# The first key tile loaded ahead of the MLP and query weights in a gated decode step

## The chip, the cores and the metric

One NeuronCore of a Trainium2 chip runs the whole program. The metric is the device time of one execution in microseconds (us). A core has five engines with their own instruction streams: PE (TensorE, matrix products into PSUM; its weight loads are listed as PEld), DVE (VectorE), ACT (ScalarE), POOL (GpSimd) and SP (SyncE), which here only issues loads. Sixteen DMA engines move data between the chip's memory (HBM) and the on-chip memory (SBUF). In this text a row of the page or of a timeline reads: line of the kernel, engine, operation, output <- inputs, shapes, count.

## The reference

One token goes through two branches, which a gate mixes. Branch A is attention over the last 4096 positions of a key and value cache with 16 key heads and 32 query heads of 128; branch B is a dense layer of 4608 with GELU.

```python
x = A_x                                           # [1, 1, 576]
g = sigmoid((x * gate_w).sum(-1, keepdims=True))
# A: W = 4096, rep = 2
q = (x @ wq).reshape(B, Sq, 32, 128).transpose(0, 2, 1, 3)
k = repeat(k_cache[:, :, Sk - W:, :], 2, axis=1)  # cache [1, 16, 32768, 128]
v = repeat(v_cache[:, :, Sk - W:, :], 2, axis=1)
p = softmax(einsum("bhqd,bhkd->bhqk", q, k) * 128 ** -0.5)
o = einsum("bhqk,bhkd->bhqd", p, v)
a = o.transpose(0, 2, 1, 3).reshape(1, 1, 4096) @ wo       # wo [4096, 576]
# B: w1 [576, 4608], w2 [4608, 576]
b = gelu(x @ w1 + b1) @ w2 + b2
return g * a + (1 - g) * b
```

All inputs and the output are bf16. Some 53.6 MB of weights and cache are read once; the output is one row of 576.

## The kernel before, in words

**Tiles and buffers.** The large loads share four SBUF buffers, named by a tag: A, B, C and D. A later tile with the same tag takes the place of the earlier one and can be loaded only when the earlier one has been read for the last time.

- A: the query weights wq (L234), then key tile 3, then value tile 2.
- B: w1 (L230), then key tile 2, then both halves of w2.
- C: key tile 0, then value tile 0, then value tile 3.
- D: key tile 1, then value tile 1, then wo.

A key or value tile holds four of the sixteen heads (`HB = 4`, so there are `NG = 4` tiles of each): 128 partitions with 128 positions of 128 numbers, 4096 KB. It is loaded by one DMA from SP in `load` (L533 to L539); each partition is one contiguous row of the cache, and the source's pattern walks 32 position blocks and 4 heads.

**The order of the loads.** SP issues in program order: w1 in two parts (L233), wq (L237), key tiles 0 to 3 (`load` called from `transpose`, L545), value tiles 0 and 1, the first half of w2 (L646), value tile 2, the small rest of wo (L651), value tile 3, wo (L752), and the second half of w2 in four parts (L757). An issue that has to wait for its buffer holds up all issues behind it. `first_load_ahead` (L48 to L59) takes the first DMA that SP has in the body of the program and puts it ahead of the barrier at the program's start, so that one load is issued at once. ACT issues four small loads of x, gate_w, b2 and b1 (L224 to L227).

**Stages.** (1) x is spread over partitions (L336 to L352) and the gate computed (L356 to L378). `y_add` (L386) starts the output sum in PSUM with the bias b2. (2) The w1 products (`moved`, L407, called at L426 and L427) and the turn of their result (`turned`, L432) give GELU and the vector `gt`. (3) The wq products (L407, called at L484), the turn `q_turned` on DVE (L487), one product (L492) and four copies on ACT (L505) put the queries into `qz_flat`. (4) For each key tile and each half f of it, DVE transposes the half in 32 by 32 blocks (`transpose`, L550) into a buffer `kt`, and PE makes 16 score products from it (`score_products`, L572). `row_max`, `exps` and `probs` (L588 to L621) make the softmax of a tile while the next one is worked on. (5) `value_products` (L662) for each value tile, with sums and the per-head output (L676 to L697). (6) The products of `gt` with w2 and of the attention output with wo (L386), two narrow casts (L828, L829), and the store (L830).

**Small buffers.** `kt_pool` has two buffers, used in turn by `rows`, `turned`, `q_turned` and then the `kt` halves. So the first `kt` half takes the buffer of `turned`, the second that of `q_turned`, and the third waits until the score products of the first are done.

**Order on the engines.** The helper `queue` (L526) ties each PE and DVE instruction from stage 4 on to the one before it, so the order on those engines is the order in which the code is written:

```python
transpose(0, 0)
scores(0, 0)
transpose(0, 1)
scores(0, 1)
for g in range(1, NG):
    transpose(g, 0)
    scores(g, 0)
    ...
```

Of the kernel before, what the change touches and what calls it, by code (L numbers as in the profile page):

```python
# [10 lines left out]
BF16 = mybir.dt.bfloat16  # L11
# [7 lines left out]
def kernel(  # L19
# [15 lines left out]
    nc = tc.nc  # L35

    P = 128
    D = 576
    Hq, Hkv, Dh = 32, 16, 128
    Sk, W = 32768, 4096  # L40
    HB = 4
    NG = Hkv // HB
    NKP = P // HB
    NCK = W // NKP
# [165 lines left out]
    big = ctx.enter_context(tc.tile_pool(name="big", bufs=1, side="right"))  # L210
# [16 lines left out]
    nc.scalar.dma_start(out=b1_t, in_=B_b1.rearrange("(h n) -> h n", h=2))  # L227


    w1_t = big.tile([P, NI, FH], BF16, name="w1_t", tag="B")  # L230
    w1_src = B_w1.rearrange("d (h n) -> (d h) n", h=2).rearrange("(p i) n -> p i n", i=NI)
    for i0, i1 in ((0, 4), (4, NI)):
# [11 lines left out]
    for base, pattern, keep in (  # L244
# [15 lines left out]
        out=is0[:], in0=low[:], scalar1=0.0, scalar2=None, op0=ALU.is_equal  # L260
# [15 lines left out]
        out=at31,  # L276
        in_=at31,
# [8 lines left out]
        out=hi5[:],  # L286
        in_=ones[:, 0:5],
# [7 lines left out]
        out=hi5[:],  # L295
        in_=hi5[:],
# [9 lines left out]
        out=hi16[:], in0=is0[:, c0 : c0 + 16], scalar1=-SCALE, scalar2=None, op0=ALU.mult  # L306
# [6 lines left out]
        out=row_of,  # L313
        in_=row_of,
# [9 lines left out]
        out=foreign[:],  # L324
        in_=foreign[:],
# [11 lines left out]
        out=xdup.rearrange("p (d t) -> p d t", t=2),  # L337
        in_=x_row.rearrange("p (d o) -> p d o", o=1).to_broadcast([1, D, 2]),
    )
    xs_ps = ps_m.tile([P, NI, 1], FP32, name="xs_ps", tag="m")  # L340
    for i in range(NI):
# [9 lines left out]
        out=x2[:, :, 0:2], in0=xs_ps[:].to_broadcast([P, NI, 2]), in1=alt, op=ALU.mult  # L351
# [5 lines left out]
        out=junk_row,  # L357
# [72 lines left out]
    for c0, src, q in ((0, h_s[0], 2), (1024, h_s[1], 2), (2048, h_m, 4)):  # L430
        n = 1024 if q == 2 else 256
        nc.vector.transpose(  # L432
            out=turned[:, c0 : c0 + n],
            in_=src[:].rearrange("p (q l j) -> p q j l", q=q, l=32),
# [13 lines left out]
    for q in range(4):  # L448
        quad = slice(32 * q, 32 * q + 32)
        nc.scalar.copy(  # L450
            out=hacc[quad], in_=hp_ps[quad, q, :, :].rearrange("p t j -> p (t j)")
# [6 lines left out]
        out=poly[:],  # L458
# [15 lines left out]
        out=gt[:], in0=hacc[:], scalar=omg[:, 0:1], in1=r_t[:], op0=ALU.mult, op1=ALU.mult  # L474
# [11 lines left out]
    for c in range(2):  # L486
        nc.vector.transpose(  # L487
            out=q_turned[:, 1024 * c : 1024 * c + 1024],
            in_=q_s[c][:].rearrange("p (h l b) -> p h b l", l=32, b=2),
# [9 lines left out]
    for b in range(4):  # L499
# [6 lines left out]
            out=diag[:, :, :, 0:8],  # L506
            in_=qj_ps[quad].rearrange("p j g q -> p g j q"),
# [18 lines left out]
    def queue(engine, emit):  # L526
        if engine in issued:
            with tc.issue_after(issued[engine].ins):
                issued[engine] = emit()
        else:  # L530
            issued[engine] = emit()

    def load(name, tag, cache, g):  # L533
        tile_ = big.tile([P, NCK, Dh], BF16, name=name, tag=tag)
        src = cache[0, HB * g : HB * g + HB, Sk - W : Sk, :].rearrange(
            "b (k c) d -> k b (c d)", k=NKP
        )
        nc.sync.dma_start(out=tile_[:].rearrange("p c d -> p (c d)"), in_=src)
        return tile_  # L539

    k_t, s_ps, kt = [None] * NG, [None] * NG, {}

    def transpose(g, f):
        if f == 0:
            k_t[g] = load("k_t", "CDBA"[g], A_k_cache, g)  # L545
        kt[g, f] = kt_pool.tile([P, SL * Dh], BF16, name="kt", tag="kt")
        keys = k_t[g][:, f * SL : (f + 1) * SL, :]
        queue(
            "dve",
            lambda: nc.vector.transpose(  # L550
                out=kt[g, f][:].bitcast(FP32),
                in_=keys.rearrange("p c d -> p (c d)").bitcast(FP32),
            ),
        )
# [63 lines left out]
    def probs(g):  # L618
# [6 lines left out]
# [9 lines that stand above are left out]
        if g > 1:  # L634
            probs(g - 2)
        row_max(g - 1)
        transpose(g, 1)
        scores(g, 1)
        exps(g - 1)
# [3 lines left out]
    w2_t = big.tile([P, NF, D], BF16, name="w2_t", tag="B")  # L643
    w2_src = B_w2.rearrange("(b p j) n -> p b j n", b=2, j=NJ)
    v_t = [load("v_t", "CD"[g], A_v_cache, g) for g in range(2)]
    nc.sync.dma_start(out=w2_t[:, 0:NJ, :], in_=w2_src[:, 0])  # L646
    v_t.append(load("v_t", "A", A_v_cache, 2))
    wo_src = A_wo.rearrange("(h d) n -> h d n", d=P)
    tail = wo_src[:, 4 * RW : P, :]
    for h0, h1, at, k in ((0, 16, 0, 4), (16, Hq, 32, 4)):  # L650
        load_tail = nc.sync.dma_start(  # L651
            out=wo_tail[at : at + h1 - h0].rearrange("h j n -> h (j n)"),
            in_=tail[h0:h1].rearrange("h j n -> h (j n)"),
# [40 lines left out]
    def outputs(g):  # L694
# [19 lines left out]
        out=ls[:],  # L714
# [22 lines left out]
        out=rgh[:],  # L737
# [15 lines left out]
        out=wo_t[:].rearrange("p r n -> p (r n)"),  # L753
        in_=wo_src[:, 0 : 4 * RW, :].rearrange("h (a r) n -> h a (r n)", a=4),
# [4 lines left out]
    def w2_rows(f0, f1):  # L759
        for f in range(f0, f1):  # L760
# [9 lines left out]
            out=om_t.rearrange("p (u h) -> p u h", u=2)[:, :, 0:16],  # L770
# [8 lines left out]
            out=om[:], in0=o_all.to_broadcast([P, Hq, 4]), in1=rgh[:, :, 0:4], op=ALU.mult  # L779
# [81 lines left out]
```

## Time and profile before

Three runs took 131.43, 131.53 and 131.67 us, median 131.53. The profiled execution took 131.67 us; the profile's span, from the first to the last recorded instruction, is 130.3 us.

| | busy us | share of the span |
|---|---|---|
| PE (matmul) | 79.3 | 61% |
| DVE | 61.0 | 47% |
| PEld (weight load) | 26.2 | 20% |
| ACT | 11.5 | 9% |
| POOL | 10.0 | 8% |
| DMA queue of SP's loads, of 16 engines | | 96.3% |

HBM was read at 412 GB/s over the span. The TensorE clock that the throttle granted was 0.82 of full speed on average. The busy shares are means over stages that have different limits; in a slice row each digit is the busy share of one fortieth of the span, in tenths. PE waited 15.1 us in all before score products, and 12.0 us before value products for their tiles to land. DVE waited 4.8 us in two pieces for key tiles.

### The profile page before, as it was taken

How to read it: one execution, taken by the hardware profiler on the slowest of the kernel's cores; microseconds unless marked ns; L12 is line 12 of the kernel's file. 1: busy time of each engine (PE TensorE's matmuls, PEld its weight loads, DVE VectorE, ACT ScalarE, POOL GpSimd, SP SyncE). 2: the span in 40 equal slices, each digit the busy share in tenths (PEclk: the TensorE clock that was granted, in tenths of full speed). 3: DMA queues.
4: the chain of work that ended last, by engine and by line, in shares of the span. 5: the costliest groups of instructions: out<-in, count | busy, mean ns of one | idle time of the engine just before them, and what ended most of it. 6: DMA issues, size and time to landing. Idle time of an engine off the chain costs nothing.

```text
span 130.3 us, 1142 instructions
## 1 busy us (share of the span) xinstructions
PE 79.3 (61%) x538; PEld 26.2 (20%) x412; DVE 61.0 (47%) x50; ACT 11.5 (9%) x27; POOL 10.0 (8%) x32
## 2 busy tenths in 40 slices
PE   0003899297106996859949946995300840789794
PEld 0003012110100221211211210132200320245572
DVE  0030006215199769999999995145900050051001
ACT  3032100300300000030003003003000000000001
POOL 7009800100000000000000000000010000000000
PEclk9999999658755799985999995599655577579999
DMA  7999999899899999989989989999989999898970
GB/s 249 404 437 432 475 419 475 364 473 473 362 453 473 408 402 473 433 382 473 443 372 473 453 362 473 391 458 443 443 372 477 444 392 475 384 493 356 407 294 15
DMA packets 2503, 53.67 MB, mean 412 GB/s; under 512 B 286, under 2 KB 418, under 8 KB 708
## 3 DMA queue, kind: packets, MB, share of 16 engines
q1 hardware_dynamic: 2490, 53.61, 96.3%
q8 instruction: 3, 0.05, 0.2%
q10 hardware_dynamic: 10, 0.01, 0.0%
HBM read 53.62 MB, written 0.00 MB: 412 GB/s over the span
## 4 chain that ended last, share of the span: by engine, by line
DMA 60%; DVE 21%; PE 13%; issue 5%; ACT 0%; DVEq 0%
DMA k_t<-in_A_k_cache_dram 31%; DMA wo_t<-in_A_wo_dram 25%; DVE kt L550 15%; PE y_ps L386 5%; PE s_ps L572 5%; DMA rows<-in_A_x_dram 5%; DVE m L588 3%; DVE pt L621 2%; PE s_ps L662 1%; PE acc L662 1%; DVE mr L591 1%; ACT out_row L828 0%; PE mt_ps L597 0%; DVE negm L605 0%; DVEq L550 0%
## 5 line engine op out<-in xcount | busy, mean ns | idle before, releaser
L572 PE MATMUL s_ps<-kt,qz_flat 128*128 128x512 bf16 x128 | 35.3, 436 | 15.1 <-DVE kt L550 8.3
L550 DVE STREAM_TRANSPOSE kt<-k_t 128x4096 f32<-128x4096 f32 x8 | 35.3, 4432 | 4.8 <-DMA k_t<-in_A_k_cache_dram 4.8
L662 PE MATMUL s_ps<-v_t,pt 128*32 128x512 bf16 x96 | 9.1, 547 | 12.0 <-DMA v_t<-in_A_v_cache_dram 12.0
L572 PEld LDWEIGHTS <-qz_flat 128*128 128x128 bf16 x64 | 7.2, 112 | 40.6 <-issue 40.4
L676 DVE TENSOR_TENSOR own<-s_ps,is 128x512 f32<-128x512 f32 x3 | 2.1, 688 | 18.9 <-PE s_ps L662 18.9
L609 ACT ACTIVATE p_t<-s_ps,negm 128x1024 bf16<-128x1024 f32 x4 | 4.5, 1114 | 50.0 <-DVE negm L605 50.0
L662 PEld LDWEIGHTS <-pt 128*32 128x32 bf16 x128 | 3.7, 117 | 17.5 <-DMA v_t<-in_A_v_cache_dram 12.2
L342 PE MATMUL xs_ps<-ident,rows 1*128 1x1 bf16 x9 | 0.6, 189 | 10.8 <-POOL ident masks.py:199 10.8
L407 PE MATMUL s_ps<-w_t,x 128*32 128x512 bf16 x36 | 6.0, 611 | 1.6 <-DVE x L350 1.6
L588 DVE TENSOR_REDUCE m<-s_ps 128x1 f32<-128x1024 f32 x4 | 4.8, 1195 | 3.9 <-PE s_ps L572 3.9
L386 PE MATMUL y_ps<-w_t,gt 128*1 128x272 bf16 (+1 forms) x72 | 6.3, 304 | 0.0
L407 PE MATMUL s_ps<-wq_t,x 128*32 128x512 bf16 x36 | 4.9, 619 | 2.2 <-DMA wq_t<-in_A_wq_dram 2.2
L621 DVE STREAM_TRANSPOSE pt<-p_t 128x1024 bf16<-128x1024 bf16 x4 | 4.9, 1224 | 2.7 <-ACT p_t L609 2.7
L432 DVE STREAM_TRANSPOSE turned<-s_ps 128x1024 f32<-128x1024 f32 x2 | 2.5, 1249 | 7.3 <-PE s_ps L407 7.2
L829 DVE CAST out_row<-y_ps 1x272 bf16<-1x272 f32 x1 | 0.4, 429 | 10.2 <-PE y_ps L386 10.2
L713 POOL TENSOR_TENSOR ls<-is,sums 128x32 f32<-128x32 f32 x1 | 0.2, 240 | 63.9 <-ACT p_t L609 63.9
L697 PE MATMUL mt_ps<-is,summed 128*128 128x8 f32 x8 | 2.0, 319 | 4.6 <-DVE summed L686 4.6
L386 PE MATMUL y_ps<-wo_t,ov 128*1 128x272 bf16 (+1 forms) x62 | 4.2, 286 | 0.8 <-DMA wo_t<-in_A_wo_dram 0.8
L356 DVE CUSTOM_DVE_ANT_0 rows<-rows 1x576 bf16<-1x576 bf16 x1 | 0.7, 746 | 8.3 <-DMA rows<-in_gate_w_dram 8.3
L386 PEld LDWEIGHTS <-gt 128*1 128x1 bf16 x72 | 4.0, 89 | 1.9 <-issue 0.7
L686 DVE TENSOR_REDUCE summed<-own 128x128 f32<-128x512 f32 x4 | 4.2, 1044 | 0.1
L487 DVE STREAM_TRANSPOSE q_turned<-s_ps 128x1024 f32<-128x1024 f32 x2 | 2.4, 1228 | 3.8 <-PE s_ps L407 3.8
(83 smaller groups left out, 51.9 us busy)
## 6 DMA issues: line engine op xcount, KB each, us to landing
k_t<-in_A_k_cache_dram SPq DMA_DIRECT2D x4, 4096.0 KB, 33.9
v_t<-in_A_v_cache_dram SPq DMA_DIRECT2D x4, 4096.0 KB, 22.8
wq_t<-in_A_wq_dram SPq DMA_DIRECT2D x1, 4608.0 KB, 25.0
wo_t<-in_A_wo_dram SPq DMA_DIRECT2D x1, 4464.0 KB
w_t<-in_B_w_dram SPq DMA_DIRECT2D x1, 2880.0 KB, 14.4
w_t<-in_B_w_dram SPq DMA_DIRECT2D x1, 2592.0 KB, 23.6
w_t<-in_B_w_dram SPq DMA_DIRECT2D x1, 2304.0 KB, 8.3
w_t<-in_B_w_dram SPq DMA_DIRECT2D x1, 1440.0 KB
```

Of the source, the lines that this page charges most:

```text
L386: last = nc.tensor.matmul(y_out[s], lhsT=vec, rhs=row[:, DH:D] if s else row[:, 0:DH], start=start, stop=stop, skip_group_check=True,)
L407: nc.tensor.matmul(last[n][32 * g : 32 * g + 32], lhsT=vec, rhs=part(n), start=start and g0 == 0, stop=g0 + 4 + g >= len(pieces), skip_gro ...
L432: nc.vector.transpose(out=turned[:, c0 : c0 + n], in_=src[:].rearrange("p (q l j) -> p q j l", q=q, l=32),)
L487: nc.vector.transpose(out=q_turned[:, 1024 * c : 1024 * c + 1024], in_=q_s[c][:].rearrange("p (h l b) -> p h b l", l=32, b=2),)
L550: lambda: nc.vector.transpose(out=kt[g, f][:].bitcast(FP32), in_=keys.rearrange("p c d -> p (c d)").bitcast(FP32),),
L572: last = nc.tensor.matmul(s_ps[g][:, u * 512 : (u + 1) * 512].rearrange("p (c k) -> p c k", k=32), lhsT=qz(g, j, 2 * f + half), rhs=kv[:, ...
L588: queue("dve", lambda: nc.vector.reduce_max(out=m1[:], in_=s_ps[g][:], axis=AX.X))
L609: nc.scalar.activation(out=p_t[:].rearrange("p c k -> p (c k)"), in_=s_ps[g][:], func=ACT.Exp, bias=negm[:, 0:1], scale=SCALE, accum_out=s ...
L621: lambda: nc.vector.transpose(out=pt[:, g, :, :].rearrange("p c q -> p (c q)"), in_=p_t[:].rearrange("p c k -> p (c k)"),),
L662: last = nc.tensor.matmul(acc[g][32 * (c % 4) : 32 * (c % 4) + 32, :], lhsT=pt[:, g, c, :], rhs=v_t[g][:, c:NCK:32, :], start=(c < 4), sto ...
L676: lambda: nc.vector.tensor_tensor(out=own[:], in0=acc[g].rearrange("p (c d) -> p c d", c=4), in1=same_c.rearrange("p (c o) -> p c o", o=1) ...
L686: lambda: nc.vector.tensor_reduce(out=summed[g][:], in_=own[:].rearrange("p c d -> p d c"), axis=AX.X, op=ALU.add,),
```

## The change

`load` is defined earlier, and key tile 0 is loaded with it ahead of w1 and wq. `transpose` loads the other three as before. Nothing else in the program's text differs.

```diff
     nc.scalar.dma_start(out=b1_t, in_=B_b1.rearrange("(h n) -> h n", h=2))
 
 
+    def load(name, tag, cache, g):
+        tile_ = big.tile([P, NCK, Dh], BF16, name=name, tag=tag)
+        src = cache[0, HB * g : HB * g + HB, Sk - W : Sk, :].rearrange(
+            "b (k c) d -> k b (c d)", k=NKP
+        )
+        nc.sync.dma_start(out=tile_[:].rearrange("p c d -> p (c d)"), in_=src)
+        return tile_
+
+    k_t = [None] * NG
+    k_t[0] = load("k_t", "C", A_k_cache, 0)
     w1_t = big.tile([P, NI, FH], BF16, name="w1_t", tag="B")
...
-    def load(name, tag, cache, g):
...
-    k_t, s_ps, kt = [None] * NG, [None] * NG, {}
+    s_ps, kt = [None] * NG, {}
 
     def transpose(g, f):
-        if f == 0:
+        if f == 0 and g > 0:
             k_t[g] = load("k_t", "CDBA"[g], A_k_cache, g)
```

SP's order becomes key tile 0, w1, w1, wq, key tiles 1 to 3, and then as before. The load that `first_load_ahead` puts ahead of the barrier is now key tile 0, and both parts of w1 are issued behind the barrier. In the program that comes out, DVE, ACT and POOL have the same instructions in the same order. On PE the products that start the output sum with b2 (L386) stand ahead of all w1 products, where before five w1 products with four weight loads stood ahead of them; there are four weight loads fewer, since weights that are still loaded are not loaded again (`keep_weights`).

More of the change, by code (lines that the diff above doesn't have):

```diff
@@ L531, in queue @@
             issued[engine] = emit()
-    def load(name, tag, cache, g):
[L534 to L539, printed above, removed]
-    k_t, s_ps, kt = [None] * NG, [None] * NG, {}
+    s_ps, kt = [None] * NG, {}
     def transpose(g, f):
-        if f == 0:
+        if f == 0 and g > 0:
             k_t[g] = load("k_t", "CDBA"[g], A_k_cache, g)
```

## The prediction

> **What bounds the kernel now.** I read the busy rows first, then the windows, then the chain of waits, then the rows of the stage that the change touches. The page's second part:
>
> ```profile
> DVE  0030006215199769999999995145900050051001
> PEclk9999999658755799985999995599655577579999
> DMA  7999999899899999989989989999989999898970
> ```
>
> The DMA row stands at 8 or 9 from the second slice to the last but two; DVE is full only in the middle. Windows give it sharply (columns: stretch, its length, busy time of PE, PEld, DVE, ACT, POOL, then clock, DMA share, GB/s):
>
> ```profile
> 0.00:0.90 0.90, 0.00 (x0) 0.00 (x0) 0.00 (x0) 0.00 (x0) 0.21 (x5) 1.00 0.00 0
> 0.90:1.10 0.20, 0.00 (x0) 0.00 (x0) 0.00 (x0) 0.00 (x0) 0.20 (x3) 1.00 2.75 553
> ...
> 4.00:124.00 120.00, 74.73 (x474) 23.08 (x350) 60.61 (x49) 9.83 (x25) 7.21 (x15) 0.80 1.00 430
> 124.00:126.00 2.00, 2.00 (x37) 1.62 (x33) 0.00 (x0) 0.00 (x0) 0.00 (x0) 1.00 0.88 353
> 126.00:128.00 2.00, 2.00 (x32) 1.30 (x29) 0.00 (x0) 0.00 (x0) 0.00 (x0) 1.00 0.29 108
> ```
>
> The transfer engines start about 1.0 us after the first issue and are then busy without a hole, at 430 GB/s, for 120 us. The chain of waits (start, length, what) tells another story until its last lines:
>
> ```profile
> 46.65 4.45 DVE kt L550
> ...
> 79.34 0.07 DVE negm L605
> 79.41 6.44 PE s_ps L572 x16
> ...
> 89.91 32.07 DMA wo_t<-in_A_wo_dram
> 121.97 0.04 issue
> 122.01 6.60 PE y_ps L386 x90
> ```
>
> wo_t is 4464 KB (KB here are 1024 bytes), which at 430 GB/s is 10.6 us of data, yet it lands 32.07 us after its issue: for 21 us it only stood behind earlier transfers. So the chain's DVE links, which release that issue, have slack, and what sets the end is the byte count: start of the stream, bytes, then the 6.6 us of y_ps products.
>
> The stage that is touched, in the timeline:
>
> ```profile
> 26.18 4.91 PE L407 MATMUL s_ps<-wq_t,x 128*32 128x512 bf16 x36 [2.22 <-DMA wq_t<-in_A_wq_dram]
> ...
> 30.67 2.38 DVE L487 STREAM_TRANSPOSE q_turned<-s_ps 128x1024 f32<-128x1024 f32 x2 [3.76 <-PE s_ps L407]
> ...
> 35.88 8.77 DVE L550 STREAM_TRANSPOSE kt<-k_t 128x4096 f32<-128x4096 f32 x2 [2.83 <-DMA k_t<-in_A_k_cache_dram]
> ...
> 40.38 8.97 PE L572 MATMUL s_ps<-kt,qz_flat 128*128 128x512 bf16 x32 [6.78 <-DVE kt L550]
> ...
> 46.65 4.45 DVE L550 STREAM_TRANSPOSE kt<-k_t 128x4096 f32<-128x4096 f32 x1 [2.00 <-DMA k_t<-in_A_k_cache_dram]
> ```
>
> DVE waits 2.83 us for key tile 0 and 2.00 us for key tile 1; between them it runs.
>
> **The change, part by part.**
>
> *Bytes.* Nothing is added or dropped. w1 (2304 + 2880 KB), wq (4608 KB) and key tile 0 (4096 KB) come in the order key, w1, w1, wq. What follows them has the same bytes ahead of it as before, so key tile 1 and every later load keep their place in the stream. One 4096 KB tile is 9.75 us at 430 GB/s; the two landings in the timeline, wq at 26.18 and key tile 0 at 35.88, are 9.70 us apart.
>
> *Landings.* The first half of w1, 8.3 us from its issue to landing before, moves to about 18.0; the second, landed at 0.80 + 14.4 = 15.2, to 24.9; wq takes key tile 0's old landing, 35.88. Key tile 0 is there at about 12, and nothing can use it: in the changed program DVE's instructions stand in the old order, its first L550 behind both L487, which need wq.
>
> *w1 stage, +9.7 us, covered.* Before, x was ready at 13.39 and the last w1 product at 22.48, 7.3 after w1's second landing; now at most 24.9 + 7.3 = 32.2, before wq's 35.88. x itself may land later than its 6.73, but no later than key tile 0 (12), and needs 13.39 - 6.73 = 6.7 us of ACT, POOL, PE and DVE after that: 18.7 at most, near w1's first landing. The only reordering on PE, the b2g pair of L386 (1.17 us) ahead of the w1 products, and four weight loads fewer, fall in that same stretch. Without wq's later landing as cover these would be a loss of their own; with it they cost nothing.
>
> *From wq to the first key transpose.* 33.05 - 26.18 = 6.87 us for products and q_turned, so L550 starts at 35.88 + 6.87 = 42.75 instead of 35.88: the 2.83 us wait is gone, a later start of 6.87 is there instead. The pair ends at 42.75 + 8.77 = 51.5.
>
> *Key tile 1.* Its transpose needs DVE (51.5), its own landing (46.6 as before) and the kt buffer of the first half, which the first 16 score products free. They start at 42.75 + 4.45 = 47.2 and took 40.38 to 45.5 = 5.1 us at a granted clock of 0.63, hence 52.3. Bounds: sixteen at the cold spacing of the 79.41 row (6.44 us) give 53.6; a warm run of 3.6 us (the x16 at 51.15) gives 51.5, DVE's own. So DVE is late by 52.3 - 46.65 = 5.6 us (4.9 to 7.0), and from there to 79.41 it was busy back to back before, so it stays late by that much.
>
> *What is late next: SP's issues.* Value tiles wait for these transposes. With the first data 1.0 us after an issue, a load must be issued 1.0 before the stream has eaten what stands ahead of it (bytes ahead / 430 GB/s + 1.0):
> - value tile 0: issued 44.7, now 51.5; 26,176 KB ahead = 63.3; needed by 62.3.
> - value tile 1: 56.9, now 62.5; needed by 72.1.
> - first half of w2: 68.1, now 73.7; needed by 81.8.
> - value tile 2: 79.4, now 85.0; 36,960 KB ahead = 89.0; needed by 88.0. Reserve 3.0 us (1.6 at the late bound).
> - value tile 3: 87.7, now 93.3; needed by 98.1. wo: 89.9, now 95.5; later still.
>
> Key tiles 2 and 3 go from 22.2 and 31.1 to about 32 and 41, needed by 43 and 53. So no queue runs dry. On PE, the value products that wait 7.72 us for value tile 2 at 101.3 just wait some 2 us. Cost of the late chain: 0, covered by 21 us of queue; without that cover it would be +5.6.
>
> *The first issue.* It is the one term that reaches the end. SP's first DMA took 396 ns to issue (w1's first half; the second 333), and data moved at about 1.0, some 0.6 after that issue ended. Key tile issues take 535 to 639 ns. If data follow the end of the issue, the stream starts 0.14 to 0.24 later; if they follow its start, 0; if a cold first issue adds again the 63 ns by which w1's exceeded its second, 0.30. A gain has no row for it: no issue on SP of such a pattern is shorter. I take 0.15.
>
> The Trainium skill (DMA: Bandwidth & Descriptors, Latency and other measured facts) gives about 600 ns to the first byte of such a queue; the trace agrees if the count starts at the issue's end (0.396 to about 1.0), and by that the shift would be 0.14 to 0.24.
>
> Sum: 0 + 0 + 0.15. The profiled execution took 131.67 (span 130.3 and 1.4 around it) and would take 131.8; it is the slowest of the three, so against the median of 131.53 I say **131.7**.
>
> **The rivals.**
>
> *The stream starts later still* (+0.3 and a little noise, 132.0): for it, the cold issue; against, that the data may follow the start of the issue. 0.16.
>
> *Value tile 2 comes too late* (slower). Place: SP's L538 at 79.4, behind DVE's last key transpose. It decides once DVE is late by over 8.6 us (88.0 - 79.4), and each us beyond is a us of empty transfer engines. Price: if PE ran cold through the six halves from 52 on, a half would take 6.44 + about 0.5 against the 5.46 of DVE's 32.8 us over six, so up to 5.6 + 8.9 = 14.5 late, 5.9 empty: 137.6; half of that, 10.1 late, is 1.5: 133.2. Against: the windows from 45.5 to 79.4 show a clock of 0.84 to 1.00 with PE just as busy. 0.12.
>
> The Trainium skill (Perfetto Trace Analysis, Optimization Strategies) would have the engines repaired for which the matmul engine waits; read so, with PE waiting 8.3 us for kt, a DVE chain 5.6 us later is a loss of 5.6, 137.1, in full. No slack is known to that rule; the 1.00 DMA share speaks against it, so it only adds to this rival's chance.
>
> *The engines' ends shift.* They do not finish together: 0.88 and 0.29 of the last two windows are 2.3 us of work each, spread evenly ending at 126.3, while some still run past 127. The page has three instruction loads on a queue of their own (0.2% of 16 x 130.3 = 4.2 us, up to 1.4 each on one engine). PE's shorter program may time them otherwise: up to 1.1 worse if one falls on a late engine (132.6, 0.07), up to 1.0 better (value 131.1, 0.12). Against: same count, same byte shares.
>
> *The two DVE waits are real gains* (2.83 + 2.00, giving 126.7): for it, the chain passes DVE; against, bytes at 430 GB/s forbid it and L487 still stands ahead. 0.03.
>
> **How the numbers follow.** Forecast 0.50, rivals 0.16, 0.12, 0.07, 0.12, 0.03. A measurement can tell some 0.2%, 0.26 us: same is 131.27 to 131.79. The forecast's own range is 131.4 to 131.9 (start shift 0 to 0.3, runs spread by 0.12 about the median); 0.04 of its 0.50 lies above 131.79. Faster 0.12 + 0.03 = 0.15; same 0.46; slower 0.04 + 0.16 + 0.12 + 0.07 = 0.39. The range 131.1 to 132.6 leaves out most of the late value tile and the gain of 126.7, and half of the improved ends.
>
> **What would show it.** Right: DMA share 1.00 at 430 from 4 to 124; first L550 at about 42.7 behind L487 without a DMA wait; third at about 52; value tile 2 issued at about 85; its products waiting some 2 us; the y_ps products at about 122.2. Wrong: any window of 2 us between 4 and 124 with a DMA share under 0.9 (a dry queue), most likely at 86 to 92; value tile 2 issued after 88; a first DMA window that opens past 1.4; a wo landing moved by more than 0.3 with the share still 1.00; or a tail longer than 6.6 us after it.

## The result and the profile after

Nine runs of the changed kernel took 131.73 to 132.22 us, median 131.94; nine of the kernel before beside them 131.31 to 131.71, median 131.53. The ratio is 1.0032, with a 95% interval of 1.0022 to 1.0041: the change costs about 0.4 us. The profiled execution took 132.13 us, its span is 130.7.

The same three rows of the page's second part, now of the changed kernel:

```profile
DVE  0003100007105998699999999956491050051001
PEclk9999999998555955999999968999985555559999
DMA  6997999989899899899899999899999999998970
```

The DVE block sits one to two slices further right; the DMA row keeps its shape, and its first digit has dropped from 7 to 6. The windows show where (columns as before):

```profile
0.90:1.10 0.20, 0.00 (x0) 0.00 (x0) 0.00 (x0) 0.00 (x0) 0.00 (x0) 1.00 0.00 0
1.10:1.50 0.40, 0.00 (x0) 0.00 (x0) 0.00 (x0) 0.00 (x0) 0.12 (x1) 1.00 2.28 573
...
4.00:124.00 120.00, 73.03 (x468) 22.79 (x340) 60.49 (x49) 9.82 (x25) 7.20 (x15) 0.83 1.00 429
124.00:126.00 2.00, 2.00 (x37) 1.73 (x34) 0.00 (x0) 0.00 (x0) 0.00 (x0) 1.00 0.98 397
126.00:128.00 2.00, 2.00 (x32) 1.28 (x30) 0.00 (x0) 0.00 (x0) 0.00 (x0) 1.00 0.41 158
```

From 0.9 to 1.1, where the kernel before already moved data, nothing moves; between 4 and 124 the share is 1.00 as before; and the engines have more left to do at the end, 0.98 and 0.41 against 0.88 and 0.29, which is 2 x (0.10 + 0.12) = 0.44 us of the 16 engines. The loss is a stream of the same length that begins later. (In windows this short the share can stand over 1; only zero or not is read from them.) The start times of the DMA packets in the trace put the first data at 1.03 us before and at 1.41 after, 0.38 later.

The chain of waits after, for its matching links:

```profile
47.44 6.06 PE s_ps L574 x16
53.50 0.02 issue
53.52 4.45 DVE kt L552
...
86.29 3.62 PE s_ps L574 x16
...
93.95 28.33 DMA wo_t<-in_A_wo_dram
122.28 0.04 issue
122.33 6.75 PE y_ps L396 x92
```

wo is issued 4 us later than before (93.95 against 89.91) and lands only 0.31 later (122.28 against 121.97): the time from issue to landing fell from 32.07 to 28.33. The queue in front of it took up the delay. The products behind that landing took 6.75 us against 6.60, which gives the rest of the 0.46 between the two profiled executions; this length varies from 6.55 to 6.77 over the traces of all the kernels here. The stage that was touched, in the timeline:

```profile
36.19 5.30 PE L417 MATMUL s_ps<-wq_t,x 128*32 128x512 bf16 x36 [3.58 <-DMA wq_t<-in_A_wq_dram]
...
40.68 2.38 DVE L497 STREAM_TRANSPOSE q_turned<-s_ps 128x1024 f32<-128x1024 f32 x2 [5.14 <-PE s_ps L417]
...
42.98 8.73 DVE L552 STREAM_TRANSPOSE kt<-k_t 128x4096 f32<-128x4096 f32 x2
...
53.52 4.45 DVE L552 STREAM_TRANSPOSE kt<-k_t 128x4096 f32<-128x4096 f32 x1 [1.81 <-PE s_ps L574]
```

The two waits of DVE for key tiles are gone; what replaced them is a wait for PE to free the kt buffer (1.81 us), and the whole chain is 6.9 us late. SP's own rows show both halves of the matter:

```profile
0.00 0.63 SPq L235 DMA_DIRECT2D k_t<-in_A_k_cache_dram  x1
1.28 0.96 SPq L243 DMA_DIRECT2D w_t<-in_B_w_dram  x2
...
86.24 0.54 SPq L235 DMA_DIRECT2D v_t<-in_A_v_cache_dram  x1
```

The first issue takes 0.63 us instead of 0.40, and value tile 2 goes out at 86.24 instead of 79.37, still ahead of the 88.4 at which the (now 0.38 later) stream needs it. The rows show a further thing: the barrier at the program's start opens later too, since SP's first DMA behind it is issued at 1.28; in the kernel before, ACT's first load, which also stands behind it, is issued at 0.79 and now at 1.28.

### The profile page after: what moved, and what is told of

Same layout as the page of the kernel before. It is cut to its first block, busy times and chain, and to the rows that moved or that the text cites. A ratio compares the mean times of both kernels' runs of the same rounds, so it can differ in the third digit from the quotient of the medians.

```text
span 130.7 us, 1139 instructions
## 1 busy us (share of the span) xinstructions
PE 78.1 (60%) x538; PEld 26.2 (20%) x408; DVE 60.9 (47%) x50; ACT 11.5 (9%) x27; POOL 10.0 (8%) x32
## 4 chain that ended last, share of the span: by engine, by line
DMA 48%; DVE 26%; PE 19%; issue 5%; SPq 1%; ACT 0%
DMA wq_t<-in_A_wq_dram 26%; DMA wo_t<-in_A_wo_dram 22%; DVE kt L552 19%; PE s_ps L574 7%; PE y_ps L396 5%; PE s_ps L417 3%; DVE m L590 3%; DVE pt L623 2%; DVE q_turned L497 2%; PE s_ps L664 1%; PE acc L664 1%; SPq L243 1%; DVE mr L593 1%; ACT out_row L830 0%; PE mt_ps L599 0%
## 5 line engine op out<-in xcount | busy, mean ns | idle before, releaser
L574 PE MATMUL s_ps<-kt,qz_flat 128*128 128x512 bf16 x128 | 33.0, 416 | 11.4 <-DVE negm L607 6.8
L417 PEld LDWEIGHTS <-x 128*32 128x32 bf16 x22 | 1.4, 115 | 18.2 <-issue 14.5
```

Source lines behind the costliest of these rows:

```text
L417: nc.tensor.matmul(last[n][32 * g : 32 * g + 32], lhsT=vec, rhs=part(n), start=start and g0 == 0, stop=g0 + 4 + g >= len(pieces), skip_gro ...
L574: last = nc.tensor.matmul(s_ps[g][:, u * 512 : (u + 1) * 512].rearrange("p (c k) -> p c k", k=32), lhsT=qz(g, j, 2 * f + half), rhs=kv[:, ...
```

## The experiments

Each ratio below is the time over that of the kernel before, measured beside it (medians 131.37, 131.40 or 131.44 us). Two theories stood against each other. A: the loss is the later first data, because of the load that is issued first. B: the loss comes from wq landing 10 us later (its products start at 36.19 instead of 26.18) and the late DVE chain behind it. Within A, two causes were open: the key tile's source pattern, which has two outer dimensions (32 position blocks by 4 heads), or the long rows of the tile.

### The first half of w1 back in front

```diff
-    k_t[0] = load("k_t", "C", A_k_cache, 0)
...
     for i0, i1 in ((0, 4), (4, NI)):
         nc.sync.dma_start(out=w1_t[:, i0:i1, :], in_=w1_src[:, i0:i1, :])
+        if i0 == 0:
+            k_t[0] = load("k_t", "C", A_k_cache, 0)
```

> The changed kernel with the first half of w1 back in front: SP's order is w1 first half, key tile 0, w1 second half, wq, and the rest as changed. Theory A (the loss is the later start of the stream, caused by which load is issued first): first DMA busy at 1.0 us as before, the DVE chain as late as in the changed kernel (third key transpose at about 53, value tile 2 issued at about 86), and the time back at 131.5 (ratio 0.999 to 1.001 to before). Theory B (the loss comes from wq landing 9.7 us later and the late DVE chain): 131.9, ratio 1.003, since nothing of that chain is given back.

Median 131.40, ratio 1.0002 (0.9989 to 1.0015). The windows and SP's rows of this run:

```profile
0.90:1.10 0.20, 0.00 (x0) 0.00 (x0) 0.00 (x0) 0.00 (x0) 0.20 (x3) 1.00 2.35 553
```

```profile
0.00 0.40 SPq L242 DMA_DIRECT2D w_t<-in_B_w_dram  x1
0.80 0.64 SPq L235 DMA_DIRECT2D k_t<-in_A_k_cache_dram  x1
...
85.42 0.54 SPq L235 DMA_DIRECT2D v_t<-in_A_v_cache_dram  x1
```

Data move from 0.9 on again. The key tile's issue is as long as ever (0.64), but in second place it is covered by the data of the first load. wq still lands behind the key tile, and the third key transpose starts at 52.71, 6.1 late: none of that shows in the time. This speaks against theory B and leaves the first issue.

### wq in front

```diff
+    wq_t = big.tile([P, NI, QH], BF16, name="wq_t", tag="A")
...
     w1_t = big.tile([P, NI, FH], BF16, name="w1_t", tag="B")
```

> The kernel before with wq ahead of w1; key tile 0 stays fourth. wq has rows of 36 KB per partition, longer than key tile 0's 32 KB, but a source pattern with one outer dimension as w1. Theory A1 (the late start comes from the key tile's source pattern of two outer dimensions): issue about 0.40 to 0.45 us, first data at 1.0 to 1.1, time 131.5 to 131.6. Theory A2 (it comes from the long rows): first data at 1.4 or later, time 131.9 or more. The DVE chain starts from key tile 0's landing at 35.9 as before in both.

Issue 0.41 us, first data at 1.02 by the packets: rows of 36 KB do not delay the start. The time is 131.54, ratio 1.0018 (0.9997 to 1.0039). The interval holds both no loss and the changed kernel's loss, so the time alone decides nothing here; the start does. The three longest of the twelve runs (132.18 to 132.86) are long outside the span, by 2.1 to 2.7 us where the others have about 1.4; the median span is 130.1 against 129.9 beside it, less apart than the changed kernel's 130.5 against 130.0 further down. Other than expected, the DVE chain came later here: the first key transpose starts at 38.30, not 35.9, and the third at 48.14.

### The key tile in front, read flat

```diff
-    k_t[0] = load("k_t", "C", A_k_cache, 0)
+    k_t[0] = big.tile([P, NCK, Dh], BF16, name="k_t", tag="C")
+    one = A_k_cache[0, 0, Sk - HB * W : Sk, :].rearrange("(p c) d -> p (c d)", p=P)
+    nc.sync.dma_start(out=k_t[0][:].rearrange("p c d -> p (c d)"), in_=one)
```

> The changed kernel, but the first key tile is read as one contiguous block of 4096 KB from head 0 (the scores of the first four heads are then of other keys): same bytes, same 32 KB rows, same place in front, a source pattern with one outer dimension. Theory A1 (the pattern with two outer dimensions delays the first data): issue about 0.40, first data at about 1.03, time 131.4 to 131.5, ratio 0.999 to 1.001, although the DVE chain is as late as in the changed kernel. Theory A2 (it is that a key tile, with its 32 KB rows, stands in front): first data at about 1.4, time 131.8, ratio 1.003.

Median 131.56, ratio 1.0006 (0.9995 to 1.0016). SP's rows, then the windows:

```profile
0.00 0.41 SPq L241 DMA_DIRECT2D k_t<-in_A_k_cache_dram  x1
...
85.80 0.54 SPq L235 DMA_DIRECT2D v_t<-in_A_v_cache_dram  x1
```

```profile
0.90:1.10 0.20, 0.00 (x0) 0.00 (x0) 0.00 (x0) 0.00 (x0) 0.20 (x3) 1.00 3.22 819
```

The tile is filled with other keys, but it has the same bytes and row length in the same place, with one outer dimension: the issue is 0.41, the data are back at 1.03, and the loss is gone within what the measurement tells, with the third key transpose still 6.4 us late (53.08). The flat source is also one stretch of memory instead of four heads far apart; the next run keeps that apart from the pattern.

### w1 in front as before, with two outer dimensions

```diff
+        if i0 == 0:
+            nc.sync.dma_start(
+                out=w1_t[:, i0:i1, :].rearrange("p i n -> p (i n)"),
+                in_=w1_src[:, i0:i1, :].rearrange("(b k) i n -> k b (i n)", b=HB),
+            )
+            continue
```

> The kernel before with one thing changed: the first half of w1, still the first load, is read with its 128 rows in another order (32 blocks by 4, as the key tile's pattern; the hidden values are then of mixed-up rows), so that its source pattern has two outer dimensions. Same bytes, same 18 KB rows, same order of loads, DVE chain as early as before. Theory A1 (that pattern in front delays the stream): issue about 0.63, first data at about 1.4, time later by 0.38, 131.8, ratio 1.003. If the pattern is not the cause: first data at 1.03 and 131.4.

Median 131.86, ratio 1.0031 (1.0021 to 1.0042). SP's rows and the windows:

```profile
0.00 0.64 SPq L234 DMA_DIRECT2D w_t<-in_B_w_dram  x1
...
79.79 0.54 SPq L544 DMA_DIRECT2D v_t<-in_A_v_cache_dram  x1
```

```profile
0.90:1.10 0.20, 0.00 (x0) 0.00 (x0) 0.00 (x0) 0.00 (x0) 0.00 (x0) 1.00 0.00 0
1.10:1.50 0.40, 0.00 (x0) 0.00 (x0) 0.00 (x0) 0.00 (x0) 0.10 (x1) 1.00 0.88 184
```

This is the counterpart: the order of before, a DVE chain only 0.4 us later (value tile 2 issued at 79.79 instead of 79.37), the same stretch of memory, and only the pattern of the first load changed, which mixes up the rows of w1. The first data come at 1.42 by the packets, and the ratio is the changed kernel's. With the flat key tile it settles the cause: the pattern with two outer dimensions on the first load, not the key tile, its size or what waits for wq. Why such a pattern takes longer, no run shows.

### The changed kernel again

> The changed kernel once more beside the one above, on the same chip: by theory A1 both are late by the same amount, first data at about 1.41 and ratio 1.003 (1.002 to 1.004).

Median 131.95 of six runs, ratio 1.0043 (1.0028 to 1.0059), a little above the expected range; issue 0.66, first data at 1.44. The interval overlaps both the first measurement and the run above.

### No head start

```diff
-    nc.at_finalize(first_load_ahead)
```

> The kernel before without the move of the first issue ahead of the barrier, so that the stream starts later by the barrier and nothing else changes. Theory A (a later start of the stream is paid one to one at the end): first data at about 1.4 to 1.8 from the start of the body's other engines' work, time later by the same amount, 0.4 to 0.8, so 131.8 to 132.2. If the end is held by something else than the stream: 131.4.

```profile
0.80 0.87 SPq L232 DMA_DIRECT2D w_t<-in_B_w_dram  x2
```

```profile
1.10:1.50 0.40, 0.00 (x0) 0.00 (x0) 0.00 (x0) 0.00 (x0) 0.40 (x5) 1.00 0.00 0
1.50:2.00 0.50, 0.00 (x0) 0.00 (x0) 0.00 (x0) 0.00 (x0) 0.50 (x5) 1.00 1.73 371
```

w1 is issued at 0.80, its first data come at 1.82 by the packets, 0.79 later than before; the time is 132.31 in five runs, ratio 1.0064 (1.0052 to 1.0076), which is 0.84 us (0.68 to 1.00) at 131.4, a little above the 0.4 to 0.8 expected. What the stream loses at its start is paid at the end, one to one within that interval. The run also answers a rival: in both kernels with the loss the barrier opens some 0.5 us later (SP's next DMA at 1.28 and 1.29), and with it the work of ACT and POOL. Here ACT's first load is issued at 0.80, as before, and the loss is still that of the stream.

### A small first load

```diff
-    for i0, i1 in ((0, 4), (4, NI)):
+    for i0, i1 in ((0, 1), (1, NI)):
```

> The kernel before with w1 cut after one of its nine rows per partition instead of four, so that the first load is 576 KB with rows of 4.5 KB. If the time to the first data hangs on the bytes or row length of the first load, data start before 1.0 and the time falls by up to 0.3, to 131.1; if it hangs on the pattern alone (theory A1), first data at about 1.0 and 131.4 to 131.5; the w1 products wait for the one large part, which is covered by DVE's waits.

First data at 1.03, 131.50, ratio 1.0012 (0.9999 to 1.0025). A load of a quarter of the size does not start sooner; nothing is won.

### The kernel before with a later DVE chain

First with the first key transpose three times:

```diff
-        queue(
-            "dve",
...
+        for _ in range(3 if (g, f) == (0, 0) else 1):
+            queue(
+                "dve",
...
```

> The kernel before with the first key transpose done three times, so that its DVE chain becomes at least as late as in the changed kernel (third key transpose at about 54 instead of 46.7, value tile 2 issued at about 86.9), with the loads in their old order. Theory A (lateness up to about 8.6 us costs nothing): 131.5, ratio 0.999 to 1.001. Theory B (the late chain is the loss): 131.9 or more, ratio 1.003 or above.

SP's row of value tile 2 in the profiled run, which took 131.63:

```profile
87.97 0.54 SPq L538 DMA_DIRECT2D v_t<-in_A_v_cache_dram  x1
```

Median 132.39, ratio 1.0062 (1.0039 to 1.0085), taken over ten runs from 131.32 to 132.97; two more took 133.34 and 133.84. Read by the letter this is theory B's number. But the chain came out later than reckoned, by 8.6 us instead of 7.5 (PE's freeing of the kt buffer, 1.91 us, comes on top), so that value tile 2 goes out at 87.97 in the profiled run, on the edge of the 88.0 at which it is needed. The wide spread would fit runs on both sides of it, but only this one has a trace, so that is not shown. That makes the run one about the edge, and it can't tell the theories apart. With the transpose twice (`range(2 ...`):

> The kernel before with the first key transpose done twice: the DVE chain about 4 us later, value tile 2 issued at about 83.5 instead of 79.4, well before the 88.0 at which it is needed. Theory A: no cost, 131.4, ratio 0.999 to 1.001, and a spread as narrow as before's, unlike the version with the transpose done three times, which issued at 88.0. Theory B (lateness costs by itself): 131.7 or more.

SP's row of value tile 2:

```profile
83.78 0.54 SPq L538 DMA_DIRECT2D v_t<-in_A_v_cache_dram  x1
```

Median 131.34, ratio 0.9991 (0.9982 to 1.0000), runs from 131.09 to 131.52. With a chain 4.4 us late and the issue 4.2 us before the edge, no cost is seen. Theory A holds, B does not.

### The changed kernel with a later DVE chain

The same edit with `range(2 ...` on the changed kernel.

> The changed kernel with the first key transpose done twice, which makes the DVE chain about 4.4 us later and changes nothing else. Theory A (the chain is hidden by the queue until value tile 2's issue passes about 88.4 us): that issue moves from 86.2 to about 90.6, the transfer engines run dry for 1 to 2.4 us around 91, time 132.8 to 134.3. Theory B (the chain sets the end at any lateness): +4.4, 136.3. If the queue had far more reserve than reckoned: 131.9.

Median 134.20 of only four runs (133.06 to 134.67), ratio 1.0197 (1.0158 to 1.0237). SP's row of value tile 2 and the windows around it:

```profile
90.56 0.54 SPq L235 DMA_DIRECT2D v_t<-in_A_v_cache_dram  x1
```

```profile
86.00:88.00 2.00, 1.49 (x9) 0.59 (x5) 2.00 (x2) 0.00 (x0) 0.00 (x0) 1.00 0.94 404
88.00:90.00 2.00, 0.00 (x0) 0.00 (x0) 2.00 (x1) 0.00 (x0) 0.00 (x0) 1.00 0.80 342
90.00:92.00 2.00, 1.42 (x5) 0.24 (x2) 0.67 (x3) 1.21 (x2) 0.00 (x0) 0.76 0.65 174
92.00:94.00 2.00, 2.00 (x7) 0.34 (x3) 1.17 (x1) 0.00 (x0) 0.00 (x0) 0.50 0.75 279
```

Here is the dry queue, in which the transfer engines have nothing left to move: the DMA share falls to 0.65 between 90 and 92. The issue is 90.56 - 88.4 = 2.2 us too late, and by the two ratios (1.0197 / 1.0032 = 1.0164) the kernel is 2.2 us slower than the changed one (some 1.7 to 2.7 by the ends of this run's interval). Of the chain's delay of 4.3 us against the changed kernel (90.56 against 86.24) only the part beyond the reserve is paid, as near as four runs tell.

No experiment beats the kernel before by more than the measurement tells. The versions with the late chain and the early start come within 0.1% of it, as one stream of fixed bytes lets expect.

## Why the prediction was right or wrong

**The bound** was right: bytes at 430 GB/s, the share 1.00 from 4 to 124 in both kernels, and a start moved by 0.79 us moved the end by 0.84.

**The landings** were right within the shift: the halves of w1 at 18.4 and 25.2 (18.0 and 24.9 said), wq at 36.15 (35.88). **The w1 stage** was covered, its last product ending near 31, ahead of wq.

**The DVE chain** was right in kind, late in size: the first key transpose at 42.98 (42.75), the third at 53.52 (52.3, bounds 51.5 to 53.6). The first sixteen score products took 6.06 us, not 5.1, since the granted clock came back to full only 5 us after they began (0.50 up to 51.5, 0.55 up to 52.5, 1.00 from there). So the chain was 6.9 late instead of 5.6, inside the 4.9 to 7.0, and value tile 2 went out at 86.24 instead of 85.0. **The cover** held, as said, with some 2 us to spare; its limit lies between 83.78 (free) and 90.56 (2.2 us paid); free too were 85.42 and 85.80 in the two versions of the changed kernel with an early start.

On PE the value products' wait for value tile 2 shrank from 7.72 to 3.98, not to 2: the last sixteen score products ran at a granted clock of 1.00 and took 3.62 instead of 6.44 (where the clock stood at 0.50 for the first 4 us), which gave 2.8 us back.

**The first issue** is the step that failed. It was named as the one term that reaches the end, and sized 0.15 with bounds of 0 and 0.30; the first data came 0.38 later. The issue alone took 0.63 against 0.40, 0.23 more, inside the reckoning. What was missed is that the time from the issue's end to the first data grows too, from 1.03 - 0.40 = 0.63 to 1.41 - 0.63 = 0.78. The prediction took that stretch as the same for every pattern. With 0.38 in its place the sum is 131.53 + 0.38 = 131.91, against 131.94 measured. The rule of about 600 ns to the first byte (the Trainium skill, DMA: Bandwidth & Descriptors, Latency and other measured facts), counted from the issue's end, fits the one-outer-dimension loads, 0.61 to 0.63 in four kernels, but not the 0.78 of the pattern with two.

**The rivals.** "The stream starts later still", 132.0 with a chance of 0.16, is what happened. The late value tile was not reached but came within about 2 us. That DVE's later chain would be paid in full did not hold: no cost is seen for 4.4 us of it, nor for 6.1 and 6.4 us with the early start. The prediction read this price out of the rule to repair what the matmul engine waits for (Perfetto Trace Analysis, Optimization Strategies, in the Trainium skill); the rule's words are the engines that block the critical path, and here DVE's chain did not block it. The shift of the engines' ends is not needed to explain anything, and no run tested it. So the likeliest case, no change, was wrong by the size of one term: with 0.38 instead of 0.15 the sum passes the 0.26 that a measurement tells. The measured 131.94 lies just above the forecast's own 131.4 to 131.9; it lies inside the stated 131.1 to 132.6 because that range also made room for the rivals. Of the prediction's signs of being wrong, the first data past 1.4 (1.41) and wo's landing moved by more than 0.3 (0.31) at a share of 1.00 came, both by little, as the late start lets expect; a third, a tail longer than 6.6 us (6.75), came without a cause that the runs show.

## What to carry to other kernels

When a stream of loads sets the time and never pauses, look at its two ends if you reorder it: at when the first byte moves, and at what follows the last one. Here the new order's only cost that was found lies at the first. A late engine behind a deep queue is free until an issue slips past the time at which the bytes ahead of it are used up, and that time can be worked out from a page of the profile (bytes ahead over the rate). Put in front the load whose pattern is cheapest to issue; here that was worth some 0.4 us of 131.5.

## What the runs showed of the hardware

A DMA whose source pattern has two outer dimensions costs more than its longer issue (0.63 to 0.66 us as the first one, against 0.40 to 0.41): the first data come at 1.41 to 1.44 instead of 1.02 to 1.03 after an idle queue, whether the rows are 32 KB or 18 KB, and the time from the issue to the data does not depend on the size (576 KB, 2304 KB, 4096 KB and 4608 KB with one outer dimension all start at 1.02 to 1.03). In second place, behind the first half of w1, the same pattern (issue 0.64) cost nothing that the measurement tells (ratio 1.0002, 0.9989 to 1.0015).
